# Attention and a mish layer on one core: the first five pairs turned by DMA alone, and reciprocal copies of one unit given to ACT

## Chip, core and metric

One core of a Trainium2 chip. The metric is device time in microseconds of one execution, lower is better. The kernel before takes 492.19 us, the median of 3 runs (490.56 to 493.78).

## What is computed

```python
scores = (1 / sqrt(64)) * q @ k.T            # 8 batches, 12 heads, 448 x 64
m = max(scores); e = exp(scores - m)
attn = e / (sum(e) + exp(-m) + 1e-9)
x = (attn @ v) -> 3584 tokens x 768
h = x @ w_in                                  # 768 x 2048
out = (h * tanh(softplus(h))) @ w_out         # 2048 x 768
```

## The kernel before

**Pairs, steps and units.** The work is cut into 48 pairs of heads (two heads of one batch; six pairs are a batch). They are counted from 0 here, as in the code. A pair has four steps. In each, PE makes scores into one of three PSUM tiles `sc` (L270 to L281), DVE takes the negated maximum of each row (`negm`, L285), and ACT takes the exponent into `en` with the row sums (`exps`, L298). A step has two 128-row tiles, the fourth step of a pair one. Scores are issued up to three steps ahead of the exponents.

**Turning and the attention output.** For the product with `v`, the exponents must be turned, so that the key index lies on partitions. A pair's `en` has four quarters j of 112 keys (padded to 128), and the turned tile is `eT` (three buffers). `normalise` issues one DMA transpose on SP's queue for it (L370). `turn_on_pe` turns a quarter on PE instead: seven 128x112 transposes into a PSUM tile (L381) and a copy of that tile to `eT` (L385, on DVE unless ACT is asked for). `av_pair` is the product with `v`, eight matmuls (L407). Its result is multiplied on DVE by the reciprocals of the denominators and goes to `xT` (L419).

**The spread reciprocals.** Before pair 12 the exponents are not divided themselves. The reciprocals are split into two bf16 parts (POOL, L322 and L323), spread over the columns by 16 small matmuls (`spread_rden`, L341) into a PSUM tile, and copied to SBUF as `rb` (L350) for the multiplication in L419. With `copy=None` that copy is ACT's and is put off: it is kept in `spread_copy` and queued when `av_pair` of the same pair is issued. With another `copy` it goes into the list `late` at once. Everything in `late` is issued by `flush_late`, which the loop calls right after the exponents of the next step.

**Two PSUM tiles for the rest.** Spreads, quarters on PE, attention outputs, the q/k transposes of the head and the layer's matmuls share two PSUM tiles, `mo`, handed out in the order in which their readers were issued (`mo_take`, `mo_free`).

**Order.** The schedule is by hand; each engine takes its instructions in program order. The head is pairs 0 to 5: in pair p, step 0 turns q and k of pair p+2, step 1 turns the last quarter of pair p-1 on PE, step 2 spreads pair p-3 and casts pair p+3, step 3 does the attention output of p-3, loads pair p+5 and issues the DMA transpose of p. After that come units u = 2, 3, ... of three pairs (u = 2 is pairs 6 to 8, u = 3 is pairs 9 to 11). A unit has 12 steps n and then eight matmul groups of the first layer with mish (`mm1_mish`, L438 and L444). From u = 4 on (`first_mm2`), the second layer's matmuls (L485) are spread between the steps. Pairs 5, 6 and 7 are turned wholly or mostly on PE (`BY_PE`); these turns are in the steps of units 2 and 3. `AV_AT` and `RDEN_AT` say at which step n of a unit the attention output and the spread of a pair stand.

**Queues.** SP issues the loads of q, k, v (three per pair, 224 KB each), the DMA transposes and the stores. POOL casts q, k, v to bf16 and issues the weights in 20 pieces (L152).

Of the kernel before, what the change touches and what calls it, by code (L numbers as in the profile page):

```python
# [19 lines left out]
def kernel(  # L20
# [9 lines left out]
    nc = tc.nc  # L30
# [5 lines left out]
    NT = 4  # L36
# [5 lines left out]
    UNITS_PER_B = HP // UNIT_PAIRS  # L42
# [284 lines left out]
    def spread_rden(p, copy=None):  # L327

        own = mo_take()
        r = own[:, :]  # L330
        hl = att[p]["hl"]
        half = SP_ * NT - 3 * 128
        for at in range(4):
            for x in range(2):
                for h in range(2):
                    if at < 3:
                        rows, c, q0 = slice(0, 128), at + 4 * h, 128 * at + half * h
                    else:
                        rows, c, q0 = slice(half * h, half * h + half), 3, 3 * 128 * (1 - h)
                    n = rows.stop - rows.start  # L340
                    nc.tensor.matmul(  # L341
                        r[h * D : (h + 1) * D, q0 : q0 + n],
                        lhsT=hl[rows, x, c : c + 1].to_broadcast([n, D]),
                        rhs=ident[rows, rows],
                        start=(x == 0), stop=(x == 1),
                    )

        def evac():
            rb[p] = rb_pool.tile([128, S], FP32, tag="rb", name="rb")
            (copy or nc.scalar.copy)(rb[p], r[:, 0:S])  # L350
            mo_free.append(own)

        if copy is None:
            spread_copy[p] = evac
        else:
            late.append(evac)

    def normalise(p, dma=True):
        st = att[p]
        en = st["en"]  # L360
        for i in range(NTILE if p >= LATE_DIV else 0):
            nc.vector.tensor_scalar(  # L362
                out=en[:, :, i, 0:SP_], in0=en[:, :, i, 0:SP_],
                scalar1=st["rden"][:, i : i + 1], scalar2=None, op0=ALU.mult,
            )
        eT = eT_pool.tile([128, NT, 2 * S], BF16, tag="eT", name="eT")
        st["eT"] = eT
        if dma:
            n = NT - 1 if p < HEAD else NT
            nc.sync.dma_start_transpose(  # L370
                out=eT[:, 0:n, :].rearrange("c j (i q) -> c (j i) q", q=128),
                in_=en[:, 0:n].rearrange("q j i c -> q (j i c)"),
            )

    def turn_on_pe(p, j, act=False):

        st = att[p]
        own = mo_take()
        ps = own[:, :].bitcast(BF16).rearrange("c (i q) -> c i q", q=128)
        for i in range(NTILE):  # L380
            nc.tensor.transpose(ps[0:SP_, i, :], st["en"][:, j, i, 0:SP_], ident)  # L381
        copy = nc.scalar.copy if act else nc.vector.tensor_copy

        def evac():
            copy(  # L385
                out=st["eT"][0:SP_, j, :].rearrange("c (i q) -> c i q", q=128),
                in_=ps[0:SP_, 0:NTILE, :],
            )
            mo_free.append(own)

        late.append(evac)
# [106 lines left out]
    first_mm2 = 2 * UNITS_PER_B  # L498
# [28 lines left out]
    HEAD = HP  # L527

    BY_PE = {HEAD - 1: 1, HEAD: 0, HEAD + 1: STEPS}
    AV_AT = {0: {6: 3, 8: 4, 10: 5}, 1: {8: 6, 10: 7, 11: 8}}  # L530
    RDEN_AT = {0: {5: 3, 7: 4, 9: 5}, 1: {7: 6, 9: 7, 10: 8}, 2: {3: 10, 7: 11}}
    TURN_BY_ACT = {(HEAD - 1, 3)}

# [15 lines left out]
    for p in range(HEAD):  # L549
        for s in range(STEPS):  # L550
            exps(p * STEPS + s)
            if s == 0 and p == 0:
                evac_qk(1, act=True)
            flush_late()
            if s == 1:
                late.extend(held)
                held.clear()
                flush_late()
            if s == 2:
                evac_qk(p + 2, act=p % 2 == 0)  # L560
            scores_ahead(HEAD * STEPS + 3)
            if s == 0:
                transpose_pair(p + 2)
                if p:
                    denominators(p - 1)
            if s == 1 and p:
                turn_on_pe(p - 1, NT - 1)
            if s in (1, 3) and p == HEAD - 1:
                load_w(1)
            if s == 2:  # L570
                if p >= 3:
                    spread_rden(p - 3)
                cast_pair(p + 3)
            if s == 3:
                if p >= 3:
                    av_pair(p - 3, hold=True)
                if p + 5 < 10:
                    load_pair(p + 5)
                normalise(p, dma=p not in BY_PE)
# [4 lines left out]
    for u in range(UNITS_PER_B, N_UNITS + 2 * UNITS_PER_B):  # L584
        attn = u < N_UNITS
        filler = deque()
        for part in plan.get(u, []):
            filler.extend(mm2_part(*part))
        total, done, acc = sum(w for _, w in filler), 0, 0.0
        p0 = u * UNIT_PAIRS  # L590
        if attn and u >= first_mm2:
            av_with.update({p0 + i: p0 + i - UNIT_PAIRS for i in range(UNIT_PAIRS)})
        end = min((u + 1) * UNIT_PAIRS, N_PAIRS) * STEPS

        for n in range(steps):
            pi, s = divmod(n, STEPS)
            p, idx = p0 + pi, p0 * STEPS + n
            late_tp = u == UNITS_PER_B and n == STEPS
            if late_tp:
                transpose_pair(p0 + 2)  # L600
            exps(idx)
            if late_tp:
                evac_qk(p0 + 2)
            if u == UNITS_PER_B + 1 and n == 0:
                for j in range(2):
                    turn_on_pe(HEAD, j)
            flush_late()
            acc += weight[n]
            want = int(total * acc / sum(weight) + 1e-6)
            while done < want:  # L610
                fn, w = filler.popleft()
                fn()
                done += w
            scores_ahead(end)
            if n in LOAD_AT:
                load_pair(p0 + LOAD_AT.index(n) + LEAD)
                cast_pair(p0 + LOAD_AT.index(n) + LEAD - 1)
            spread = RDEN_AT.get(u - UNITS_PER_B, {})
            if n in spread:
                spread_rden(spread[n], copy=None if u == UNITS_PER_B else nc.vector.tensor_copy)  # L620
            early = AV_AT.get(u - UNITS_PER_B)
            if early is not None:
                if n in early:
                    av_pair(early[n])
                for pe, n0 in BY_PE.items():
                    first = 2 if pe == HEAD else 0
                    if pe // UNIT_PAIRS == u - 1 and n0 + first <= n < n0 + NT:
                        turn_on_pe(pe, n - n0, act=(pe, n - n0) in TURN_BY_ACT)
            elif s == (2 if pi else 0) and N_PAIRS <= p < N_PAIRS + UNIT_PAIRS:
                av_pair(p - UNIT_PAIRS)  # L630
            if u - UNITS_PER_B < len(W_AT):
                load_w(W_AT[u - UNITS_PER_B].get(n, 0))
        assert done == total

        moe = u < N_UNITS + UNITS_PER_B
        b, w = (u - UNITS_PER_B) // UNITS_PER_B, u % UNITS_PER_B
        nxt = p0 + UNIT_PAIRS
        todo = sorted(range(p0, nxt), key=lambda p: p in BY_PE)
        for f in range(FF_U):
            if moe:  # L640
                mm1_mish(b, w * FF_U + f)
            if u == UNITS_PER_B and f in (2, 6) or u == UNITS_PER_B + 1 and f == 1:
                load_w(1)
            if not attn:
                continue
            if f == 0:
                denominators(p0, UNIT_PAIRS)
                for p in todo if p0 < LATE_DIV else todo[:1]:
                    normalise(p, dma=p not in BY_PE)
            if f == 5 and u == UNITS_PER_B + 1:  # L650
                spread_rden(p0, copy=nc.scalar.copy)
            if f == 4:
                scores_ahead(min(nxt * STEPS + 1, N_PAIRS * STEPS))
            if f in (1, 3, 5):
                transpose_pair(nxt + f // 2, bank=f // 2 % 2)
                evac_qk(nxt + f // 2)
            if f >= FF_U - 2:
                scores_ahead(min(nxt * STEPS + f - FF_U + 4, N_PAIRS * STEPS))
            if f in (3, FF_U - 1) and p0 >= LATE_DIV:
                p = todo[1 + f // (FF_U - 1)]  # L660
                normalise(p, dma=p not in BY_PE)
# [32 lines left out]
```

## Time and profile before

| | |
|---|---|
| median of 3 runs | 492.19 us |
| profiled execution | 488.69 us, span 486.9 us, granted clock 0.987 |
| busy in the span | PE 93%, DVE 74%, ACT 71%, POOL 21% |
| chain that ended last | PE 75%, ACT 11%, DVE 8%, DMA 2% |
| head, 14.5 to 43.7 us | PE 22.0, DVE 25.5, ACT 25.9 of 29.2 us; DMA share 1.14 |
| steps of unit 2, 43.7 to 61.3 us | PE 13.5, DVE 13.6, ACT 15.6 of 17.6 us; DMA share 1.16 |
| steps of unit 3, 73.1 to 91.6 us | PE 12.7, DVE 16.0, ACT 16.3 of 18.5 us; DMA share 1.01 |

The profiled execution is one run; its time is the span and 1.8 us around it. Busy times of an engine are summed over its instructions in the stretch. The DMA share is the time of all packets over 16 engines' time; packets in flight together count twice, so a full stretch shows somewhat over 1. Times of the chain and the timeline are microseconds from the start of the span.

### The profile page before, as it was taken

To read this page: it belongs to the slowest core of one execution; us is meant where nothing else is said; L and a number is where in the kernel's file an instruction comes from. 1 tells how busy PE (TensorE), PEld (TensorE's weight loads), DVE (VectorE), ACT (ScalarE), POOL (GpSimd) and SP (SyncE) were. 2 spreads that over 40 slices of the span, in tenths; PEclk is the share of its full clock that TensorE was granted. 3 is DMA by queue.
4 is the path that set the end of the run, shared out by engine and by line. 5 is a ranking of instruction groups with operands and counts; after the bars stand their busy time and mean duration, and the time that the engine had idled before them with its cause. 6 is when DMAs were issued, how large, how long until landed. Compare 5 with 4: busy or idle time off the path is not lost.

```text
span 486.9 us, 9223 instructions
## 1 busy us (share of the span) xinstructions
PE 453.3 (93%) x3219; PEld 258.4 (53%) x3219; DVE 359.4 (74%) x713; ACT 345.4 (71%) x905; POOL 103.4 (21%) x184
## 2 busy tenths in 40 slices
PE   4676896898999999999999999999999999999996
PEld 2344454554655565555555555555555555556563
DVE  4889738758889898889899888889898978520011
ACT  5998859677687887879687868788797968412300
POOL 4534535206013030403012120404040200000000
PEclk9999798999999999999999999999999999999999
DMA  8999999999998979799999998998979886761122
GB/s 233 221 235 206 265 197 241 145 185 246 143 220 224 204 195 197 230 194 258 164 247 174 221 209 190 223 199 223 199 236 164 210 152 142 146 146 31 36 59 72
DMA packets 204975, 91.08 MB, mean 187 GB/s; under 512 B 161792, under 2 KB 201472, under 8 KB 204928
## 3 DMA queue, kind: packets, MB, share of 16 engines
q1 hardware_dynamic: 197440, 84.20, 79.5%
q0 software_dynamic: 7488, 6.29, 9.0%
q8 instruction: 25, 0.41, 0.4%
q14 instruction: 22, 0.18, 0.1%
HBM read 45.61 MB, written 11.01 MB: 116 GB/s over the span
## 4 chain that ended last, share of the span: by engine, by line
PE 75%; ACT 11%; DVE 8%; DMA 2%; issue 2%; SPq 1%; POOL 0%; DVEq 0%; ACTq 0%
PE mo L438 26%; PE mo L485 24%; ACT en L298 9%; PE sc L264 7%; DVE negm L285 6%; PE sc L407 5%; PE sc L438 4%; PE sc L186 3%; PE mo L407 2%; DMA k_f<-in_k_dram 1%; PE mo L341 1%; PE sc L270 1%; DMA v_f<-in_v_dram 1%; SPq L125 1%; DVE eT L385 1%
## 5 line engine op out<-in xcount | busy, mean ns | idle before, releaser
L298 ACT ACTIVATE en<-sc,negm 128x448 bf16<-128x448 f32 x336 | 208.4, 641 | 22.6 <-DVE negm L285 20.7
L285 DVE TENSOR_REDUCE negm<-sc 128x2 f32<-128x896 f32 x192 | 183.0, 971 | 44.8 <-PE sc L264 28.2
L485 PE MATMUL mo<-w_out_sb,gT 128*128 128x384 bf16 (+1 forms) x1024 | 166.7, 306 | 0.0
L438 PE MATMUL mo<-xT,w_in_sb 128*128 128x448 bf16 x672 | 141.9, 353 | 0.5 <-DVE xT L417 0.3
L485 PEld LDWEIGHTS <-gT 128*128 128x128 bf16 x1024 | 96.3, 98 | 55.4 <-issue 1.3
L444 ACT ACTIVATE gT<-mo 128x448 bf16<-128x448 f32 x112 | 59.6, 543 | 83.0 <-PE mo L438 82.7
L438 PEld LDWEIGHTS <-w_in_sb 128*128 128x128 bf16 x768 | 72.7, 98 | 63.6 <-issue 3.3
L166 POOL CAST q_bf<-q_f 112x512 bf16<-112x512 f32 x47 | 29.3, 623 | 230.8 <-DMA q_f<-in_q_dram 208.0
L362 DVE TENSOR_SCALAR en<-en,rden 128x448 bf16<-128x448 bf16 x252 | 73.6, 365 | 0.8
L264 PE MATMUL sc<-kT,qd 128*128 128x448 bf16 x252 | 71.6, 354 | 0.0
L298 ACT ACTIVATION_READ_ACCUMULATOR en<-sc,negm 128x1 f32 x336 | 71.1, 212 | 0.0
L472 DVE COPY o_sb<-mo 128x384 f32<-128x384 f32 (+1 forms) x64 | 32.1, 501 | 48.3 <-PE mo L485 48.1
L264 PEld LDWEIGHTS <-qd 128*128 128x128 bf16 x252 | 24.6, 97 | 28.8 <-issue 12.9
L407 PE MATMUL sc<-eT,v_bf 112*64 112x448 bf16 x288 | 34.1, 357 | 2.1 <-ACT en L298 1.6
L223 DVE TENSOR_SCALAR qd<-sc 64x448 bf16<-64x448 bf16 x72 | 27.7, 385 | 7.5 <-PE sc L186 6.6
L407 PEld LDWEIGHTS <-v_bf 112*64 112x64 bf16 x384 | 20.9, 111 | 22.3 <-issue 15.6
L168 POOL CAST v_bf<-v_f 112x512 bf16<-112x512 f32 x48 | 29.9, 624 | 12.2 <-DMA v_f<-in_v_dram 11.5
L167 POOL CAST k_bf<-k_f 112x512 bf16<-112x512 f32 x47 | 29.1, 619 | 9.1 <-DMA k_f<-in_k_dram 8.0
L270 PE MATMUL sc<-kT,qd 64*128 64x448 bf16 x36 | 15.8, 457 | 7.7 <-ACT en L298 7.2
L186 PEld LDWEIGHTS <-q_bf 112*128 112x128 bf16 x192 | 14.3, 103 | 15.4 <-DVE q_bf L166 4.2
L231 ACT COPY kT<-sc 128x448 bf16<-128x448 bf16 x39 | 20.8, 534 | 0.6 <-PE sc L186 0.6
L438 PE MATMUL sc<-xT,w_in_sb 128*128 128x448 bf16 x96 | 20.8, 353 | 0.0
(53 smaller groups left out, 279.2 us busy)
## 6 DMA issues: line engine op xcount, KB each, us to landing
q_f<-in_q_dram SPq DMA_DIRECT2D x48, 224.0 KB, 5.3
k_f<-in_k_dram SPq DMA_DIRECT2D x48, 224.0 KB, 5.4
v_f<-in_v_dram SPq DMA_DIRECT2D x48, 224.0 KB, 5.5
w_in_sb<-in_moe_w_in_dram POOLq DMA_DIRECT2D x12, 256.0 KB, 7.3
w_out_sb<-in_moe_w_out_dram POOLq DMA_DIRECT2D x8, 384.0 KB, 7.4
out_dram<-o_sb SPq DMA_DIRECT2D x7, 336.0 KB, 3.5
out_dram<-o_sb SPq DMA_DIRECT2D x8, 288.0 KB, 5.0
out_dram<-o_sb SPq DMA_DIRECT2D x8, 240.0 KB, 3.5
```

Of the source, the lines that this page charges most:

```text
L166: cast_q(out=q_bf, in_=q_f.rearrange(by_t, t=NT))
L167: cast_k(out=k_bf, in_=k_f.rearrange(by_t, t=NT))
L168: nc.gpsimd.tensor_copy(out=v_bf, in_=v_f)
L264: nc.tensor.matmul(sc[:, bk, 0:S], lhsT=qT[:, i].rearrange("d h r -> d (h r)"), rhs=kT, start=True, stop=True,)
L285: nc.vector.tensor_reduce(out=negm, in_=sc[:, 0 : len(cols), 0:S], axis=AX.X, op=ALU.max, negate=True)
L298: e = nc.scalar.activation(out=st["en"][:, :, c, 0:SP_], in_=sc[:, bk, 0:S].rearrange("q (j c) -> q j c", j=NT), func=AF.Exp, bias=st["neg ...
L362: nc.vector.tensor_scalar(out=en[:, :, i, 0:SP_], in0=en[:, :, i, 0:SP_], scalar1=st["rden"][:, i : i + 1], scalar2=None, op0=ALU.mult,)
L407: nc.tensor.matmul(av[h * 64 : (h + 1) * 64, 0:S], lhsT=v_bf[:, h, j * D : (j + 1) * D], rhs=e_h, start=(j == 0), stop=(j == NT - 1),)
L438: nc.tensor.matmul(h_ps[:, 0:S], lhsT=w_in_sb[:, dm, ff * 128 : (ff + 1) * 128], rhs=xT[b][:, dm, :], start=(dm == 0), stop=(dm == DM_T - 1),)
L444: nc.scalar.activation(out=gT[:, ff, b % 2 * S : b % 2 * S + S], in_=h_ps[:, 0:S], func=AF.Mish)
L472: nc.vector.tensor_copy(out=o_sb[:, cols], in_=st["o"][:, 0:n_cols])
L485: nc.tensor.matmul(st["o"][:, 0:n_cols], lhsT=gT[:, ff, i * 128 : (i + 1) * 128], rhs=w_out_sb[:, ff, cols], start=(ff == 0), stop=(ff == ...
```

## The change

Two edits. In the head, the DMA transposes of pairs 0 to 4 take all four quarters (28 blocks of 128x128 instead of 21), and `turn_on_pe` for their last quarter is gone. In unit 3 (pairs 9 to 11, the tenth to twelfth), the three copies `rb` of pairs 6, 7 and 8 are made by ACT instead of DVE and are put off to the attention output of their pair, and the attention outputs of pairs 7 and 8 stand at steps 9 and 10 instead of 10 and 11.

```diff
         if dma:
-            n = NT - 1 if p < HEAD else NT
             nc.sync.dma_start_transpose(
-                out=eT[:, 0:n, :].rearrange("c j (i q) -> c (j i) q", q=128),
-                in_=en[:, 0:n].rearrange("q j i c -> q (j i c)"),
+                out=eT.rearrange("c j (i q) -> c (j i) q", q=128),
+                in_=en.rearrange("q j i c -> q (j i c)"),
             )
...
-    AV_AT = {0: {6: 3, 8: 4, 10: 5}, 1: {8: 6, 10: 7, 11: 8}}
+    AV_AT = {0: {6: 3, 8: 4, 10: 5}, 1: {8: 6, 9: 7, 10: 8}}
     RDEN_AT = {0: {5: 3, 7: 4, 9: 5}, 1: {7: 6, 9: 7, 10: 8}, 2: {3: 10, 7: 11}}
...
-            if s == 1 and p:
-                turn_on_pe(p - 1, NT - 1)
...
             if n in spread:
-                spread_rden(spread[n], copy=None if u == UNITS_PER_B else nc.vector.tensor_copy)
+                spread_rden(spread[n], copy=None if u < first_mm2 else nc.vector.tensor_copy)
```

## Prediction

> **What bounds the kernel now.** I read the table of engines and the chain first, then the chain in order of time over the two stretches that the change touches, then who waited for whom there, then DMA. From 91.6 us on the chain is mostly PE (L438, L485), and the change adds nothing there. So the question is when PE may start the first layer of unit 2 (61.30) and of unit 3 (91.57); what is won or lost before these points is carried to the end.
>
> In the head ACT is busy 25.9 of 29.2 us and the chain runs through ACT and DVE. The chain in order of time, and ACT's waits between 8 and 62 us (total, times, longest):
>
> ```profile
> 19.04 0.27 DVE eT L385
> ...
> 29.77 0.54 DVE eT L385
> ...
> 41.91 0.54 DVE eT L385
> 42.45 0.04 issue
> 42.49 0.72 PE mo L341 x16
> ...
> 43.28 0.53 ACT rb L350
> ```
>
> ```profile
> ACT en L298 <- DVE negm L285: 3.4, 3, 2.4
> ACT rb L350 <- PE mo L341: 2.3, 3, 1.6
> ```
>
> The reader sees the copy of the turned quarter (L385) on the path of every pair: it holds back the next maximum on DVE, or it holds a `mo` tile for which the spread (L341) waits, and behind it ACT's copy of `rb`. The longest, 1.63 us before 43.28, is exactly this: copy to 42.44, spread to 43.2, ACT.
>
> DMA is the other thing full in the head: its share is 1.14 over 14.5 to 43.7. The last of the five transposes is issued at 43.52; the view of DMA issues for that moment gives its time to landing, the timeline what it is for:
>
> ```profile
> eT<-en SPq DMA_TRANSPOSE x1, 11.6
> ```
>
> ```profile
> 58.35 0.95 PE L407 MATMUL mo<-eT,v_bf 112*64 112x448 bf16 x8
> ```
>
> So pair 4's turn lands at 43.52 + 11.6 = 55.1 and is read at 58.35: 3.2 us of slack. The others have more: pair 1 lands at 32.2 and is read at 38.1, pair 2 at 37.8 (read 43.4), pair 3 at 45.8 (read 55.1).
>
> In unit 3's last steps DVE is full and the chain goes DVE, PE, then the layer. The timeline there:
>
> ```profile
> 86.94 0.62 DVE L350 COPY rb<-mo 128x448 f32<-128x448 f32 x1
> 87.47 0.62 DVE L385 COPY eT<-mo 112x896 bf16<-112x896 bf16 x1
> 87.61 0.95 PE L407 MATMUL mo<-eT,v_bf 112*64 112x448 bf16 x8 [0.67 <-DVE rb L350]
> ...
> 88.59 0.62 DVE L419 TENSOR_TENSOR xT<-mo,rb 128x448 bf16<-128x448 f32 x1
> ...
> 89.27 0.70 PE L341 MATMUL mo<-ident,hl 128*64 128x128 bf16 x16 [0.20 <-DVE xT L419]
> ...
> 91.57 2.44 PE L438 MATMUL mo<-xT,w_in_sb 128*128 128x448 bf16 x12
> ```
>
> **Head: what is removed.** Five times seven transposes on PE (0.99 us a time up to 34 us, 0.55 after) and five copies on DVE (0.61 each, 0.54 to the next instruction). I walk ACT's row, pair by pair. Pair 2: the wait of 0.79 at 21.20 is for a maximum behind the copy; without the copy the maximum ends 0.54 earlier: 0.5 won. Pair 4: spread 0 no longer waits for the copy (0.38) and for the slot that the quarter took on PE, so `rb` comes right after the exponents (its 0.35 of idle goes); with the maximum held up likewise, about 0.5 more. Pair 5: the 0.29 before 36.65, and of the 1.63 before 43.28 about 1.2, because the spread can run at about 40 and only its own 0.7 and the put-off copy remain. Sum 2.3; the ceiling is all of ACT's idle time, 29.2 - 25.9 = 3.3, the floor nothing. ACT would begin unit 2 at about 41.4 instead of 43.71, and the output of pair 4 could start at 58.35 - 2.3 = 56.0.
>
> **Head: what is added.** Seven blocks per transpose are 7 x 128 x 128 x 2 bytes = 229 KB. No row shows their price by itself. A 28-block transpose with nothing beside it, in a late stretch, gives the rate:
>
> ```profile
> 401.80:406.10 4.30, 4.30 (x28) 2.36 (x28) 3.97 (x6) 3.37 (x11) 0.00 (x0) 1.00 1.17 222
> ```
>
> At 222 GB/s 229 KB are 1.04 us, five times 5.2 us, all ahead of pair 4's landing because loads and transposes follow one another in SP's queue. From below, DMA had room: the share is 0.91 over 24.5 to 27, 0.76 over 36.5 to 39.5 and 0.96 over 43 to 47, where a stretch full of loads shows 1.11 (56.4 to 58.3). That is 2.5 x 0.18 + 3 x 0.32 + 4 x 0.14 = 2.0 us that a longer queue can fill. So pair 4 lands 3.2 us later (5.2 - 2.0), at 58.3; the ends are 0 (all in gaps, and the issue on SP's queue takes 4.0 to 4.5 us for 21 blocks undisturbed and 4.2 for 28) and 7.0 (three at 1.04, and the two that share the engines with weights at 1.94: pair 4's 21 blocks took 5.8 us of packets). The other four stay ahead of their readers: pair 2's, the tightest, lands at 37.8 + about 3.0 against 41.1.
>
> **Where they meet.** From pair 4's output to the first layer the chain is output 0.95, L419 0.62, output of pair 5 0.95 (it takes the `mo` tile that L419 frees), with handoffs 2.6 us. The layer starts at max(56.0, 58.3) + 2.6 = 60.9 instead of 61.30: 0.4 won. Of the 2.3 won by ACT, 1.9 turn into a wait of PE for DMA; queued behind that wait are spread 5, output 5 and the layer, but no scores, since the unit's last scores are issued before. Break-even is a landing at 58.7.
>
> Behind it on SP's queue stand the loads of pairs 10 to 12; the k of pair 12 was issued at 55.16, just after the landing, and goes about 3 us later. POOL's casts wait for these loads (4.9 us before 55.72 already) and its weight pieces stand behind the casts. I cost this at nothing: pair 10's q and k are turned at 66.4 and their cast would end near 62.5; the DMA share falls to nearly nothing between 87 and 89, which takes up what is left. If that cover fails, the last w_out piece of the first half comes late for L485 at 105 us, where its landing has some 2 us to spare: about 1 us.
>
> **Unit 3.** Three copies of 0.62 leave DVE and come to ACT at 0.54. If DVE's time were the path, this would win 1.9; if all three went onto ACT's path, it would lose 1.6. Walking it: pair 6's output now takes the tile of the last quarter of pair 7, free when that copy ends; the copy moves up to 86.94 and ends at 87.55, and the output starts at 87.6 as before. ACT now has: exponents of step 9 to 86.77, `rb` 6 to 87.3, step 10 to 88.55; `rb` 7 waits for its spread, which stands behind output 6 on PE and ends near 89.1, so `rb` 7 ends at 89.65 and the exponents of step 11 wait behind it (88.65 before). On PE: output 7 after L419 of pair 6, 89.25 to 90.2; spread 8 to 90.9; output 8 after L419 of pair 7, 90.9 to 91.85; layer at 91.87 instead of 91.57. So 0.3 lost: the chain of outputs and L419 through two tiles stays, and the tile handed over by ACT is no earlier. The table load for mish then ends near 92.8, just before the first group ends.
>
> **Sum.** -0.4 + 0.3 = -0.1 on a span of 486.9, that is an execution of 488.6 against 488.69. The median of the runs lies 3.5 us above the profiled one, so I carry the difference to it: 492.1. A difference of 1%, 4.9 us, is about what a measurement of this kernel can tell from no change.
>
> **Rivals.** (1) DMA has room and the landing stays before 56.0: then the whole 2.3 arrives, with unit 3 between -1.9 and +0.3: 488.0 to 490.2, say 489.5. For it: SP's issue times do not grow with the blocks. Against: loads and transposes stand back to back from 16 to 62 us at a share of 1.15. (2) Slower: DMA falls further behind than the gaps can take, pair 4's output waits for it, and the layer with it. It decides from a landing at 58.7. With no gap filled it lands at 60.3 and costs 1.6; at 7.0 late, 62.1 and 3.4; with unit 3's 0.3 that is 494.1 to 495.9, say 495. For it: the share, and the weights that ran beside two of the transposes. Against: the 2.0 us of gaps. (3) PE's clock. Scores take 0.55 us before 34 us, 0.36 from there to 47.7, behind the unbroken burst of spread and output at 30 to 34, and 0.55 again from 47.8 to 51.8, where the granted clock is 0.57. With the quarters gone PE may stay slow through pairs 4 and 5: 4 x 0.19 for scores, 0.4 for a spread, 0.76 for an output and 0.23 for the q/k turns are 2.15 us a pair, 4.3 in all; that makes PE's 5.8 us a pair the bound over ACT's 5.3, so the 2.3 are not won and about 1 is lost besides, but the slots of pair 4's output are then late anyway: 492.5 to 493.5. The Trainium skill, in TensorE: Matmul & The Clock Gate, Part 1, says that the array's clock is halved until a window of about 3.4 us was busy, and again after an idle one; the rows agree with it as far as they go. (4) That nothing of this happens is not possible: the instructions are gone.
>
> **How the numbers follow.** Forecast (within 1.5 us of 492.1) 0.50, rival 1 0.17, rival 2 0.20, rival 3 0.13. The range takes in rivals 1 and 2, with 0.5 either way for the run: 488.5 to 496.0. Its own range for the forecast is 490.6 to 493.6. Faster by over 1% (below 487.3) needs more than rival 1: 0.04. Slower by over 1% (above 497.1) needs rival 2 and the late weights together: 0.07. Within 1%: 0.89.
>
> **What would show it.** Right: no L385 on the chain before 43 us; ACT at pair 6 near 41.4; PE idle before pair 4's L407, released by DMA; that L407 near 58.3; the transposes of the head landing later one by one; unit 3's layer 30 to 31 us after unit 2's, as before. Wrong: pair 4's output waiting for nothing (rival 1) or starting after 58.7 (rival 2); scores of 0.55 us between 34 and 47 us (rival 3); DVE, not the handing over of `mo`, setting the end of unit 3.

## The result, and the profile after

The changed kernel takes 495.49 us (median of 22 executions, 490.39 to 500.68), the kernel before, measured beside it, 491.34 us (22 executions, 489.63 to 497.83). The ratio is 1.0058, 95% interval 1.0032 to 1.0084: some 3 us slower. Every ratio here leaves out executions over 1.5% above the fastest of their kernel, six of the changed kernel's and one of the other's, while the medians are of all executions and differ by 4.2 us. The profiled execution, 500.34 us with a span of 498.6, is one of the longest of these, so it shows the loss larger than it usually is; a shorter one, of 492.35 us, is among the experiments.

From L370 on the changed kernel's lines are one lower: the attention output is L406, the DMA transpose L369, the two layers L437 and L484.

**What came as computed.** ACT's waits in the head, 8 to 44 us:

```profile
ACT en L298 <- DVE negm L285: 2.8, 3, 2.4
ACT rb L350 <- PE mo L341: 1.0, 1, 1.0
```

The copy of the turned quarter is gone from the chain, and the waits for `negm` and for the spread, 3.4 and 2.0 us in the same stretch before, fall to 2.8 and 1.0. The last `rb` of the head is at 41.36 us (43.28 before). PE's timeline (start, length, what, idle time before it and its cause), at pair 4's output and at the first layer of unit 2 and of unit 3:

```profile
57.69 0.95 PE L406 MATMUL mo<-eT,v_bf 112*64 112x448 bf16 x8 [0.82 <-DMA eT<-en]
...
60.31 2.44 PE L437 MATMUL mo<-xT,w_in_sb 128*128 128x448 bf16 x12
...
91.31 2.44 PE L437 MATMUL mo<-xT,w_in_sb 128*128 128x448 bf16 x12
```

The output of pair 4 waits 0.82 us for its transpose, and the two layers start 0.99 and 0.26 us earlier than before (61.30 and 91.57). So up to 91 us nothing is lost between these two executions.

**Where it is lost.** ACT loads its exponent table at the start of a unit's steps and its mish table at their end, so these loads mark the stages. For unit 4, after and then before:

```profile
103.83 1.28 ACT L298 ACT_TABLE_LOAD   x1
133.31 1.28 ACT L443 ACT_TABLE_LOAD   x1
```

```profile
104.09 1.28 ACT L298 ACT_TABLE_LOAD   x1
121.67 1.28 ACT L444 ACT_TABLE_LOAD   x1
```

The steps of unit 4 take 29.48 us instead of 17.58. That is +11.9, and the span is 11.7 longer (498.6 against 486.9). What follows the second load is 365.3 against 365.2 us. The page, the waits of 100 to 125 us (total, times, longest), and the chain in order of time name the cause:

```profile
PE 71%; DMA 13%; ACT 8%; DVE 5%; issue 1%; SPq 0%; POOL 0%; DVEq 0%
...
L484 PE MATMUL mo<-w_out_sb,gT 128*128 128x384 bf16 (+1 forms) x1024 | 170.1, 309 | 8.5 <-DMA w_out_sb<-in_moe_w_out_dram 8.5
```

```profile
PE mo L484 <- DMA w_out_sb<-in_moe_w_out_dram: 8.5, 4, 4.9
```

```profile
93.16 23.29 DMA w_out_sb<-in_moe_w_out_dram
...
116.49 0.80 PE mo L484 x2
```

The second layer (L484) waits for the `w_out` pieces, 8.5 of the 11.9 us; how the rest comes about isn't worked out here. DMA's share of the chain is 13% (2% before). SP's queue shows how they became late (start, how long the issue held the queue). After, then before:

```profile
62.14 13.74 SPq L369 DMA_TRANSPOSE eT<-en  x1
75.98 0.53 SPq L125 DMA_DIRECT2D q_f<-in_q_dram  x1
...
87.99 33.81 SPq L369 DMA_TRANSPOSE eT<-en  x3
```

```profile
60.74 5.53 SPq L370 DMA_TRANSPOSE eT<-en  x1
66.36 0.55 SPq L125 DMA_DIRECT2D q_f<-in_q_dram  x1
...
88.64 18.91 SPq L370 DMA_TRANSPOSE eT<-en  x3
```

And POOL, after and then before (in brackets, idle time and cause):

```profile
61.27 0.61 POOL L166 CAST q_bf<-q_f 112x512 bf16<-112x512 f32 x1 [5.44 <-DMA q_f<-in_q_dram]
...
67.32 1.46 POOL L152 DMA_DIRECT2D w_in_sb<-in_moe_w_in_dram  x2
...
85.75 0.61 POOL L166 CAST q_bf<-q_f 112x512 bf16<-112x512 f32 x1 [14.59 <-DMA q_f<-in_q_dram]
...
89.98 2.24 POOL L152 DMA_DIRECT2D w_out_sb<-in_moe_w_out_dram  x3
```

```profile
55.72 0.61 POOL L166 CAST q_bf<-q_f 112x512 bf16<-112x512 f32 x1 [4.91 <-DMA q_f<-in_q_dram]
...
73.99 0.61 POOL L166 CAST q_bf<-q_f 112x512 bf16<-112x512 f32 x1 [7.12 <-DMA q_f<-in_q_dram]
...
78.73 2.24 POOL L152 DMA_DIRECT2D w_out_sb<-in_moe_w_out_dram  x3
```

Read from top to bottom. (1) The longer transposes of the head delay the loads behind them, so the cast at 55.72 stands at 61.27. (2) The five weight pieces behind the casts go out at 63.5 to 71.2 instead of 57.6 to 66.9. All five are issued while pair 8's transpose, issued at 62.14, holds SP; before, three were. And the transpose now stands 0.5 us behind the last load instead of 4.4. (3) It holds SP for 13.74 us instead of 5.53 and lands 22.8 us after its issue instead of 11.2. (4) The loads of pair 13 stand behind it: 75.98 instead of 66.36. (5) The cast that needs them is at 85.75 instead of 73.99, and three `w_out` pieces wait behind it on POOL: 89.98 instead of 78.73. (6) Before, they went out 9.9 us ahead of the transposes of pairs 9 to 11; now they go out 2.0 us behind the first of them and run beside them (SP held 33.81 us instead of 18.91). The median time from issue to landing of a `w_out` piece between 60 and 130 us is 20.2 us (7.4 before), of a transpose 21.7 (9.5).

### The profile page after: what moved, and what is told of

Its sections match the earlier page's. It is cut to its first block, busy times and chain, and to the rows that moved or that the text cites. A ratio compares the mean times of both kernels' runs of the same rounds, so it can differ in the third digit from the quotient of the medians.

```text
span 498.6 us, 9145 instructions
## 1 busy us (share of the span) xinstructions
PE 458.2 (92%) x3184; PEld 257.0 (52%) x3184; DVE 355.5 (71%) x705; ACT 346.6 (70%) x908; POOL 103.4 (21%) x184
## 4 chain that ended last, share of the span: by engine, by line
PE 71%; DMA 13%; ACT 8%; DVE 5%; issue 1%; SPq 0%; POOL 0%; DVEq 0%
PE mo L484 24%; PE mo L437 23%; ACT en L298 8%; PE sc L264 8%; DMA eT<-en 6%; PE sc L406 6%; DMA w_out_sb<-in_moe_w_out_dram 5%; DVE negm L285 4%; PE sc L437 3%; PE sc L186 3%; DMA k_f<-in_k_dram 2%; PE mo L406 1%; PE sc L270 1%; PE mo L341 1%; PE mo L380 1%
## 5 line engine op out<-in xcount | busy, mean ns | idle before, releaser
L298 ACT ACTIVATE en<-sc,negm 128x448 bf16<-128x448 f32 x336 | 208.5, 641 | 33.8 <-DVE negm L285 32.1
L484 PE MATMUL mo<-w_out_sb,gT 128*128 128x384 bf16 (+1 forms) x1024 | 170.1, 309 | 8.5 <-DMA w_out_sb<-in_moe_w_out_dram 8.5
L437 PE MATMUL mo<-xT,w_in_sb 128*128 128x448 bf16 x672 | 141.8, 352 | 0.3 <-DVE xT L416 0.3
L484 PEld LDWEIGHTS <-gT 128*128 128x128 bf16 x1024 | 97.0, 99 | 66.7 <-issue 8.6
L437 PEld LDWEIGHTS <-w_in_sb 128*128 128x128 bf16 x768 | 72.7, 98 | 63.3 <-issue 3.0
L406 PE MATMUL sc<-eT,v_bf 112*64 112x448 bf16 x288 | 34.9, 363 | 0.9 <-ACT en L298 0.5
L406 PEld LDWEIGHTS <-v_bf 112*64 112x64 bf16 x384 | 21.0, 113 | 23.4 <-issue 16.2
L270 PE MATMUL sc<-kT,qd 64*128 64x448 bf16 x36 | 17.2, 488 | 9.9 <-ACT en L298 9.2
L437 PE MATMUL sc<-xT,w_in_sb 128*128 128x448 bf16 x96 | 20.8, 353 | 0.0
## 6 DMA issues: line engine op xcount, KB each, us to landing
w_out_sb<-in_moe_w_out_dram POOLq DMA_DIRECT2D x8, 384.0 KB, 19.3
```

Of the source, the lines that this page charges most:

```text
L298: e = nc.scalar.activation(out=st["en"][:, :, c, 0:SP_], in_=sc[:, bk, 0:S].rearrange("q (j c) -> q j c", j=NT), func=AF.Exp, bias=st["neg ...
L406: nc.tensor.matmul(av[h * 64 : (h + 1) * 64, 0:S], lhsT=v_bf[:, h, j * D : (j + 1) * D], rhs=e_h, start=(j == 0), stop=(j == NT - 1),)
L437: nc.tensor.matmul(h_ps[:, 0:S], lhsT=w_in_sb[:, dm, ff * 128 : (ff + 1) * 128], rhs=xT[b][:, dm, :], start=(dm == 0), stop=(dm == DM_T - 1),)
L484: nc.tensor.matmul(st["o"][:, 0:n_cols], lhsT=gT[:, ff, i * 128 : (i + 1) * 128], rhs=w_out_sb[:, ff, cols], start=(ff == 0), stop=(ff == ...
```

## Experiments

All ratios are to the kernel before on the same chip, with 95% intervals. The first four separate the parts of the change. In the expectations, e1 to e12 are the first parts of the runs' names.

**Head alone.** The changed kernel with unit 3 as before.

```diff
-    AV_AT = {... 1: {8: 6, 9: 7, 10: 8}}
+    AV_AT = {... 1: {8: 6, 10: 7, 11: 8}}
-  spread_rden(spread[n], copy=None if u < first_mm2 else nc.vector.tensor_copy)
+  spread_rden(spread[n], copy=None if u == UNITS_PER_B else nc.vector.tensor_copy)
```

> Only the head's edit: pairs 0 to 4 turned wholly by DMA; unit 3 as before. Theory D (the added DMA blocks push loads, casts and weight pieces late, and the second layer's matmuls of unit 4 wait for w_out): the whole loss is here, 2 to 5 us over the kernel before, PE waits for w_out near 105 us. Theory U (the loss is unit 3's, ACT handing over the PSUM tiles): 0.5 to 1.5 us faster than before, and no wait for w_out. Theory C (PE's clock stays low in the head): also slower by 1 to 3 us, but with scores of 0.55 us between 34 and 47 us and without the wait for w_out.

Measured: 1.0023 [0.9991, 1.0055], median 493.75 against 492.48. That is less than theory D had, and in this profile PE waits in unit 4 not for `w_out` but 3.4 us for the transposes of pairs 9 to 11. It leans to the slow side, and with unit 3 (next) at nothing the head is where to look; but the interval holds 1, so this run alone decides nothing.

**Unit 3 alone.** The kernel before, with the same lines the other way round.

> Only unit 3's edit: copies of the spread reciprocals by ACT and outputs of pairs 7 and 8 a step earlier; head as before. Theory D: within 0.5 us of before (my walk gave 0.3 slower). Theory U: 2 to 4 us slower, with the layer of unit 3 that much later behind the layer of unit 2. Theory C: as before.

Measured: 1.0005 [0.9977, 1.0032]. By itself this edit can't be told from nothing. The spacing of the first layers of units 2 and 3 says the same: 31.00 us in this profile and in the changed kernel's, 30.27 in the profile of before and 30.62 in two later kernels without the edit (e9, e11), so 0.4 to 0.7 us are lost, too little for the ratio to show.

**Head's gain without its transfers.** The changed kernel with 21 blocks in the head; the last quarter of pairs 0 to 4 isn't turned, and their outputs sum three quarters, which is two matmuls fewer a pair.

```diff
+            n = NT - 1 if p < HEAD else NT
-                out=eT.rearrange(...), in_=en.rearrange(...)
+                out=eT[:, 0:n, :].rearrange(...), in_=en[:, 0:n].rearrange(...)
...
-        for j in range(NT):
+        nj = NT - 1 if p < HEAD - 1 else NT
+        for j in range(nj):
```

> Both edits, but the DMA transposes of pairs 0 to 4 keep 21 blocks and the last quarter is turned by nobody; the attention output of these pairs sums three quarters (two matmuls fewer a pair). This has the gain in the head without the added blocks. Theory D: 1 to 2.5 us faster than before, no wait for w_out. Theory U: 2 to 4 us slower than before minus the head's 2, so 0 to 2 slower. Theory C: slower than before as the changed kernel is, for PE has still less to do.

Measured: 0.9935 [0.9901, 0.9969], median 489.04 against 492.48, with no wait for `w_out`. It is somewhat faster than theory D had.

**Head's transfers without its gain.** The kernel before with 28 blocks; PE still turns the quarter, and the copy goes to a part of `gT` that isn't read before it is written anew.

```diff
-                out=eT[:, 0:n, :].rearrange(...), in_=en[:, 0:n].rearrange(...)
+                out=eT.rearrange(...), in_=en.rearrange(...)
...
-                out=st["eT"][0:SP_, j, :]
+                out=(gT[:, FF_T - 1, :] if p < HEAD - 1 else st["eT"][:, j, :])[0:SP_, :]
```

> The kernel before, with 28 blocks in the DMA transposes of pairs 0 to 4 while PE still turns the last quarter, whose copy goes to a place that nobody reads. This has the added blocks without the gain in the head and without unit 3's edit. Theory D: 3 to 7 us slower than before, more than the changed kernel, with the wait for w_out in unit 4. Theory U: as before within 1 us. Theory C: as before within 1 us, since PE has the same work.

Measured: 1.0094 [1.0058, 1.0129], median 496.55 against 492.48. The wait for `w_out` in unit 4 is there, 1.3 us. (In this profile the first layer of unit 2 also starts 3.0 us later than in that of before, but so it does, by 2.9, in e2, which has no added blocks.) So the five times seven blocks are the loss, and the missing PE work (with e3's missing matmuls, and with unit 3's edit) is a gain of 0.65%. From e3 to the changed kernel it is 1.2%, some 6 us, for the blocks, where the prediction had let 1.9 us of ACT's gain go to them.

Next came the place. If the queue's order were all (loads of pair 13 behind a long transpose), issuing these loads first would cure it.

**Loads of pairs 13 and 14 ahead of pair 8's transpose,** in the changed kernel and in the kernel before:

```diff
-        if p >= N_PAIRS:
+        if p >= N_PAIRS or p in loaded:
...
+                if u == UNITS_PER_B:
+                    load_pair(13)
+                    load_pair(14)
                 # then normalise, with pair 8's transpose
```

> The changed kernel, with the loads of pairs 13 and 14 issued on SP's queue ahead of pair 8's DMA transpose instead of behind it. Theory D, chain version (pair 8's transpose runs beside a bunch of weight pieces, takes 18 us instead of 6 and blocks SP's queue, so the casts of pair 13 and the w_out pieces behind them come late): the cast of pair 13 no longer waits 14 us, the w_out pieces land before 105 us, no wait for them; 1 us faster to 1 us slower than the kernel before, against 3 us slower for the changed kernel. Theory D, volume version (DMA simply has 5 us more to do before unit 4, whatever the order): still 2 to 4 us slower than before, w_out as late.

> The control: the same reordering of loads in the kernel before. Chain version: 0 to 2 us faster than before, since some executions of it meet the same bunching. Volume version: as before within 1 us.

Measured: 1.0132 [1.0089, 1.0175] in the changed kernel, 1.0019 [0.999, 1.0049] in the one before. The cure failed: the kernel is slower than either version of the expectation had it. The wait of L484 for `w_out` is gone, but pair 8's transpose now holds SP for 20.38 us from 66.88 on, and its output waits (waits of 60 to 130 us):

```profile
PE mo L406 <- DMA eT<-en: 7.2, 1, 7.2
```

In the kernel before it is 19.33 us and a wait of 2.5. So the order on SP is only one half: the transpose itself is slow while loads and weights are in flight.

**Only pairs 0 and 1 turned wholly by DMA,** the rest as in the kernel before: 14 more blocks, not 35.

```diff
-            n = NT - 1 if p < HEAD else NT
+            n = NT - 1 if 2 <= p < HEAD else NT
...
-            if s == 1 and p:
+            if s == 1 and p > 2:
                 turn_on_pe(p - 1, NT - 1)
```

> The kernel before, with only pairs 0 and 1 turned wholly by DMA and their quarters gone from PE; pairs 2 to 4 and unit 3 as before. Volume version: two fifths of the loss of the head's edit, 0.5 to 1.5 us slower. Chain version: within 1 us of before, as the pieces shift by only 2 us; the head's gain for these two pairs is some 0.5 us.

Measured: 0.9963 [0.9929, 0.9997], median 490.05 against 491.95. That is faster than either version had it: with fewer blocks part of the gain is kept, the steps of unit 4 take 17.2 us, and nothing waits for `w_out`.

**Weight pieces held until pair 8's transpose has landed,** in the changed kernel, in the kernel before, in e7 and in e1. A two-element copy on POOL reads what the transpose wrote, and the weights queue behind it.

```diff
-    W_AT = ({1: 1, 5: 1, 9: 1}, ...
+    W_AT = ({1: 1}, ...
...
-            if u == UNITS_PER_B and f in (2, 6) or u == UNITS_PER_B + 1 and f == 1:
+            if u == UNITS_PER_B + 1 and f == 1:
...
                 # behind normalise, with pair 8's transpose
+                if u == UNITS_PER_B:
+                    nc.gpsimd.tensor_copy(out=seen, in_=att[8]["eT"][:, 0, 0:2])
+                    load_w(4)
```

> The changed kernel, with weight pieces 6 to 9 held back on POOL until pair 8's DMA transpose has landed (POOL copies two of its elements first), so that it runs without weights beside it. Chain version: that transpose takes 5 to 7 us instead of 18, the loads of pair 13 follow by 70 us, w_out comes in time: within 1.5 us of the kernel before. If the transpose is slow for another reason than the weights beside it, it stays over 12 us and the kernel is 3 us slower or more.

Measured: 0.9984 [0.9949, 1.002], median 490.5 against 491.95 (one of its 12 executions took 1575.78 us, which nothing here explains). SP's timeline and POOL's wait in 60 to 130 us:

```profile
62.31 8.17 SPq L370 DMA_TRANSPOSE eT<-en  x1
```

```profile
POOL seen L649 <- DMA eT<-en: 5.7, 1, 5.7
```

With both edits in place, the transpose holds SP for 8.17 us instead of 13.74 and lands 10.2 us after its issue instead of 22.8 (the "18 us" of the expectations is neither figure). There is no wait for `w_out`, the steps of unit 4 take 17.2 us, and the loss is gone, though DMA moves the same bytes as in the changed kernel. So the loss needs this collision, not the volume alone: the place is shown.

> The control of the held-back weights: the kernel before with weight pieces 6 to 9 behind the landing of pair 8's transpose. In the theory as it stands now (what costs is transposes and weight pieces in flight together, in the changed kernel nearly always, in the kernel before by chance) this removes its chance cases: 0 to 2 us faster than before, and a narrower spread. If the hold is a gain by itself, whatever the collisions, it wins as much here as in the changed kernel, 3.6 us.

Measured: 0.9989 [0.9955, 1.0024]. The hold by itself brings nothing measurable, so in e8 it didn't add a gain of its own but took the collision away. The spread is narrower, as expected: 490.46 to 493.3 us in 12 executions, against 488.55 to 499.68 in 29 of the kernel before.

> Pairs 0 and 1 wholly by DMA, the others and unit 3 as before, and weight pieces 6 to 9 held back. The head's gain for two pairs (0.5 to 1) with less DMA than the changed kernel and no collision with pair 8: 2 to 4 us faster than the kernel before, the fastest of the set. If the gain of the two pairs run without the hold was chance, within 1 us of the kernel before.

> The head's edit alone with the held-back weights: unit 3 as before. If unit 3's edit costs nothing when DMA is out of the way: within 1 us of the run with both edits and the hold. If it costs what the step from the head alone (1.0023) to both edits (1.0058) suggests, 1.7 us faster than that run.

Measured: 0.9946 [0.9909, 0.9983] with two pairs (487.46 to 490.87 in all 12 executions) and 0.9942 [0.9904, 0.9981] with five (two groups: nine at 487.5 to 492.3, three at 495.7 to 497.5; the median of all twelve is 489.01, against 491.75 for the kernel before). Both beat both kernels; e10 is the steadier one. The profiled execution of e11 was one of the three, and there the second layer waits 7.3 us for `w_out`: the second collision, of `w_out` and the transposes of pairs 9 to 11, can still happen without the first.

**The changed kernel once more,** unedited, for another execution.

> The changed kernel once more, unedited, to see another of its executions. In the profiles so far everything behind the steps of unit 4 is equal to 0.1 us (365.2 us), and the steps of unit 4, from ACT's table load for the exponents to the one for mish, take 17.2 us where SP holds the three transposes of pairs 9 to 11 for 18 to 23.5 us, 18.6 to 21.0 at 26 to 27 us, 26.1 at 32.2 and 29.5 at 33.8. Theory (the late w_out pieces and the transposes beside them are the loss, and their size differs between executions): the profiled execution follows this row. At 493 to 497 us the transposes are held for 25 to 31 us and the steps take 19 to 24; at 491 or less, below 24 us and 17.2 to 17.6. Rival (the slow parts of the changed kernel are elsewhere, and the 29.5 was the accident of one execution): the steps of unit 4 take 17.2 to 17.6 us though the execution is above 493.5. Ratio as before: 1.003 to 1.009.

Measured: 1.0089 [1.0039, 1.0138]; the profiled execution is 492.35 us. Its SP queue and PE's waits from 84 to 135 us:

```profile
89.15 25.63 SPq L369 DMA_TRANSPOSE eT<-en  x3
```

```profile
PE sc L406 <- DMA eT<-en: 2.5, 1, 2.5
```

Here the transposes hold SP for 25.63 us, the outputs that need them wait 2.5, and the steps of unit 4 take 20.3 us. That is between the two cases that the expectation named, and on its row; the rival (17.2 to 17.6 us there) isn't borne out, though the execution is not above 493.5, where it was to be decided. The rest behind unit 4 is 365.3 us again; over all profiles it is 364.8 to 366.6, less exact than the expectation had it. All kernels with the loads in the old order together, by how long SP was held for pairs 9 to 11:

| kernel | held, us | PE waits in unit 4 for `w_out`, `eT` | steps of unit 4, us |
|---|---|---|---|
| e10 | 18.0 | none | 17.2 |
| before | 18.9 | none | 17.6 |
| e3 | 19.0 | none | 17.2 |
| e9 | 20.1 | none | 17.6 |
| e7 | 21.6 | none | 17.2 |
| e8 | 23.5 | none | 17.2 |
| e12 (the changed kernel) | 25.6 | 0, 2.5 | 20.3 |
| e1 | 26.2 | 0, 3.4 | 21.0 |
| e4 | 26.7 | 1.3, 1.1 | 20.4 |
| e2 | 26.8 | 1.2, 0.6 | 18.6 |
| e11 | 32.2 | 7.3, 0 | 26.1 |
| after | 33.8 | 8.5, 0 | 29.5 |

Up to 23.5 us the hold costs nothing. From 25.6 on the unit waits for it. That e2, whose head is that of the kernel before, stands in the lower half shows that the collision is not new: in that execution the cast of pair 13 was at 83.61 (73.99 in the profile of before). The change makes it usual.

## Why the prediction was wrong, and where it was right

**Head, removed: right.** ACT was to begin unit 2 at about 41.4; the last `rb` is at 41.36 and the exponents follow at 41.79 (43.71 before). So 1.9 of the 2.3 us came, between these two executions.

**Head, added, up to pair 4: about right in the landing, not in its parts.** The transpose was to land at 58.3, 3.2 us later than before; it lands at 57.64, 2.5 later. PE's wait for it was the mark to look for, and it is there, 0.82 us. The layer starts at 60.31 (60.9 predicted). But this small delay is the difference of two larger figures. The transpose goes out 5.9 us later (49.44 against 43.52), mostly because those of pairs 0 to 3 hold SP 0.8 to 2.2 us longer each, and it lands 8.2 us after its issue instead of 11.6. So the gaps that were to take up 2.0 us didn't shorten SP's queue: the k of pair 12 goes out 4.8 us later (59.94 against 55.16), where the prediction had about 3.

**Unit 3: right in sign and about in size.** 0.3 lost was predicted; the layers stand 30.80 to 31.00 us apart with the edit (the changed kernel, e2, e8) and 30.27 to 30.63 without (before, e1, e4, e7, e9, e11), so 0.2 to 0.7 are lost. Two profiles lie outside: e3 with 32.13 (with the edit) and e10 with 31.64 (without).

**The sum up to 91 us: right, in part by luck.** -0.1 was predicted, and the layer of unit 3 is 0.26 us earlier. But these are two single executions, and the head's length differs more between executions than the terms of this sum. Where the head is that of before, the first layer of unit 2 starts at 60.87 (e6), 61.30 (before), 64.21 (e2) and 65.25 us (e9); with the changed head at 59.83 to 63.18 us (the changed kernel, e1, e5, e8, e11, e12). The profile from which the prediction was worked out is one of the quick ones. In the two late ones the scores between 34 and 47 us take 0.55 us in part (e2) or throughout (e9), in the two quick ones 0.35 to 0.36.

**The step that failed** is the one costed at nothing: the loads behind pair 4's transpose, the casts and the weight pieces. Three things in it were wrong. First, it said that the fall of the DMA share between 87 and 89 would take up what is left. But idle DMA time doesn't help an instruction that stands behind another in a queue, and the step walked SP's queue only to pair 12. The next thing on it is pair 8's transpose, and behind that the loads of pair 13. Second, it kept that transpose at the price it had before, though the delay put it right behind the loads and beside all five weight pieces (landing 22.8 us after its issue, 11.2 before). Third, "about 1 us" if the cover fails: the first three `w_out` pieces were issued 11.2 us later in the profiled execution, and the steps of unit 4 lost 11.9; in the shorter execution (e12) they lost about 3. By the ratio it is some 3 us net, with the gain of the head in it.

**Rival 2** gave about the measured time (495), but hardly by its mechanism. Pair 4's output starts at 56.64 to 57.69 in the profiles of the changed kernel and of e5, e8, e11 and e12, after 0.8 to 3.75 us of waiting; only in e1, at 59.02, does it pass the break-even of 58.7, and there the layer starts at 63.18, later than in the profile of before (though not than in e2 and e9). So its place may cost something in some executions, and the rival was right that DMA falling behind is what costs. But it is in unit 4, with the late weights and the transposes beside them, that the changed kernel's own profiles lose; the late weights were priced at about 1 us and costed at nothing in the sum. **Rival 1** fell with them, and what spoke for it, that SP's issue times do not grow with the blocks, didn't hold (0.8 to 2.2 us more each). But its size, 489.5, is about what the kernel reaches when the collision is taken away (490.5 and 489.01 in e8 and e11).

**Rival 3, the clock,** showed its mark in part, but the mark isn't the change's. In the first profile of the changed kernel, scores take 0.35 to 0.36 us from 33 to 39 us and 0.53 to 0.55 from 39.7 to 47 us; the granted clock over 34 to 47 us is 0.71 (1.00 before). In its second profile (e12) they take 0.35 to 0.36 us up to 45 us, and the clock is 1.00. And e9, whose head is that of before, has 0.55 us throughout at 0.50. The granted clock doesn't settle the speed either: e4 has 0.55 us throughout at 1.00. The Trainium skill (TensorE: Matmul & The Clock Gate, Part 1) has the clock halved after an idle window; which windows counted as idle no run here shows. The clock is not the main cause: e12 has the quick scores and still loses about 3 us in unit 4 (20.3 against 17.2 to 17.6), and in the first profile the whole loss lies behind 91 us.

**What stays open:** why a transpose beside weights loses so much more than the weights' own share. In the Trainium skill (DMA: Bandwidth & Descriptors, Queues, rings and completion order) each DMA engine takes turns between the queues that have work, a packet at a time. The rows fit this in that two queues in flight slow each other (pair 8's transpose lands in 22.8 us with the weights beside it, in 10.2 with them held, e8), but no run here separates it from another limit. Nor is it shown why the transpose lands in 11.2 us in the profile of before, with three pieces beside it, and in 17.4 to 19.2 in e3, e2 and e7, or what makes the same head some 4 us longer in one execution than in another. It isn't settled either whether unit 3's edit adds to the collision: e1 with 1.0023 and the changed kernel with 1.0058 have intervals that overlap, and so have e11 and e8.

## What to carry to other kernels

When a transfer in a full queue grows, follow the queue past the first reader: list what is issued behind it, which engine's queue waits for that, and which transfers stand behind *that*, until the delay meets a real gap in the same queue. Free DMA time is no gap if the late transfer can't be issued. And where transfers of two queues are in flight together, a shift of one queue can put it beside the other: take half of such a change first (two pairs wholly by DMA gave 0.9963 [0.9929, 0.9997], the whole change 1.0058 [1.0032, 1.0084]), or let the less urgent queue wait for the other's landing. Last, look at more than one execution before a sum of tenths is read off a profile: here a head that wasn't changed differed by some 4 us.

## What the runs showed of the hardware that was not expected

- The time of pair 8's DMA transpose (28 blocks) from issue to landing went with what was in flight: 7.7 to 10.2 us where the weights wait for it (e8 to e11), 11.2 in the profile of before, 17.4 to 22.8 in the other profiles with weight pieces beside it (e3, e2, e7, e4, e1, the changed kernel), 29.0 and 30.6 with six loads issued just ahead of it as well (e6, e5). It holds SP's queue for a part of this: 5.1 to 8.2 us, 5.5, 6.3 to 13.7, and 19.3 and 20.4. While it is held, nothing behind it is issued.
- Seven blocks more lengthened the hold of the head's first four transposes by 0.8 to 2.2 us each (4.0 to 4.5 us for pairs 1 to 3 before, 5.0 to 6.7 after). Added up, this put the issue of pair 4's 5.9 us later, while its own time to landing fell from 11.6 to 8.2 us.
- PE's speed in the head differed between executions of one kernel: the granted clock over 34 to 47 us was 0.71 in one profile of the changed kernel and 1.00 in the other; with the head of before it was 1.00, 0.87 and 0.50 (before, e2, e9).
